# The second product of a token MLP: order of the wide, low and narrow matmuls within a step

## Chip, cores and metric

The kernel runs on one core of a Trainium2 chip. The metric is the device time of one execution in microseconds; the median of three runs stands for a kernel.

## What is computed

The block is a pre-norm layer: linear attention with a learned feature map, then an MLP across the tokens. With x of 2048 tokens by 512 channels:

```python
h = x + A(layernorm(x))            # attention, 32 heads of 16
n = layernorm(layernorm(h))        # one norm of the block, one of the MLP
u = gelu(n.T @ w1 + b1)            # (512, 1792): w1 is (2048, 1792)
y = u @ w2 + b2                    # (512, 2048): w2 is (1792, 2048)
out = h + y.T
```

The change lies in `u @ w2`, the last stage.

## The kernel before, in words

The work comes in three stretches: attention with its projections, the first product of the MLP (it starts while attention still runs), and the second product from about 379 us on.

The second product is written as Winograd's form of Strassen's method: a block of two by two becomes seven products of sums and differences instead of eight. The blocks on the one side are halves of a 256-row piece of w2 by two token tiles; on the other side they are halves of the matching piece of u by two halves of 256 channels. `STEPS` (line 767) runs over 8 token pairs `sp` and, in each, 7 pieces `p` of the hidden dimension. So a token pair has seven steps, and a step has seven products, listed in `PROD` (line 817) as (slice of the weights, slice of u, bank, half). For the last token pair `LAST` (line 819) is used.

Every operand is split in two parts, a high one, rounded to the type `float32r` that the matmuls take, and a low one with what is missing. A product needs high by high, high by low and low by high. The tile of u holds high and low beside each other, 256 columns each. So where `half` is None, one matmul of 512 columns does high weights by both parts (line 823, here called wide), and one of 256 columns adds low weights by the high part (line 824, here called low). Where `half` is 0 or 1 the two results of a wide matmul shall be added to one half of a bank at once, and three matmuls of 256 columns are used (line 827, here called narrow). In `PROD` five products are of the first kind and two, both in the third bank, are narrow: sixteen matmuls a step. In `LAST` all seven are narrow, 21 a step.

`products` (line 830) takes a list of steps: for each product it goes through the steps. The first five steps of a token pair are issued one by one; the sixth and seventh (the last three in the last pair) are issued together, product by product, so that the banks are finished one after the other (line 861). Behind them ACT and DVE add the banks up and GpSimd's queue adds the result to the output in memory.

The weights arrive by a DMA on the SP queue two steps at a time (`load_w2`, line 775). DVE makes the sums (lines 785 to 787), ACT the high part of all seven slices in one instruction (line 796, three buffers `whi`), DVE the low part (line 805, two buffers `wlo`). These are issued at the head of each group of two steps, for groups further ahead. The parts of u lie in `un` for the first two pieces and in `uf` for the others. The order of TensorE, DVE and ACT is the order of the code (line 839); each engine waits only where its operands or buffers make it wait. There are eight banks, and a token pair takes six in turn.

Of the kernel before, what the change touches and what calls it, by code (L numbers as in the profile page):

```python
# [22 lines left out]
NP = NF // 2  # L23
# [13 lines left out]
def block_kernel(ctx: ExitStack, tc: tile.TileContext, x, xT, wT, phic, wo, w1, b1, w2, b2,  # L37
                 kvmask, ident_in, out):
    nc = tc.nc
# [685 lines left out]
    U, UB, far = {}, {}, {}  # L725
# [43 lines left out]
    RAW, WH, AW = {}, {}, {}  # L769
# [7 lines left out]
    def sums_w2():  # L777

        g = done["sums"]
        if g == NGR:  # L780
            return
        done["sums"] += 1
        load_w2(g)
        raw = RAW[g]
        nc.vector.tensor_add(raw[:, 0:2], raw[:, 1].unsqueeze(1).to_broadcast([P, 2, GRP * P]), raw[:, 2:4])
        nc.vector.tensor_add(raw[:, 5], raw[:, 1], raw[:, 2])
        nc.vector.tensor_add(raw[:, 6], raw[:, 4], raw[:, 5])

    def hi_w2():

        g = done["hi"]
        if g == NGR:
            return
        done["hi"] += 1
        WH[g] = ws.tile([P, 7, GRP * P], F32R, name="whi", bufs=3)
        nc.scalar.activation(WH[g], RAW[g], AF.Copy)  # L796

    def lo_w2():

        g = done["lo"]  # L800
        if g == NGR:
            return
        done["lo"] += 1
        wl_ = ws.tile([P, 7, GRP * P], F32R, name="wlo", bufs=2)
        nc.vector.tensor_sub(wl_, RAW[g], WH[g])  # L805
        for i, step in enumerate(STEPS[g * GRP:(g + 1) * GRP]):
            AW[step] = WH[g][:, :, i * P:(i + 1) * P], wl_[:, :, i * P:(i + 1) * P]
# [10 lines left out]
            (4, 3, 5, None))  # L818
    LAST = ((2, 1, 0, 0), (5, 5, 0, 1), (0, 0, 1, 0), (1, 4, 1, 1), (3, 6, 2, 0), (6, 2, 2, 1), (4, 3, 3, 0))

    def product(o, half, a, b, first, start, stop):
        if half is None:
            nc.tensor.matmul(o, a[0], b, start=start, stop=stop, skip_group_check=True)  # L823
            nc.tensor.matmul(o[:, 0], a[1], b[:, 0], start=False, stop=stop, skip_group_check=True)  # L824
            return
        for i, (x, y) in enumerate(((0, 0), (0, 1), (1, 0))):
            nc.tensor.matmul(o[:, half], a[x], b[:, y], start=start and first and i == 0, stop=stop and i == 2,  # L827
                             skip_group_check=True)

    def products(sp, ps, order):  # L830
        for a, b, bk, half in order:
            for p in ps:
                wh_, wl_ = AW[sp, p]
                product(bank[bk], half, (wh_[:, a], wl_[:, a]), UB[p, b], half != 1, p == 0, p == NP - 1)

    def flat(a):
        return a.rearrange("p k d -> p (k d)")
# [3 lines left out]
    for n, (sp, p) in enumerate(STEPS):  # L841
        t = 2 * sp
        last = t + 2 == NT
        if n % GRP == 0 and p < NP - 1:
            lo_w2()
            hi_w2()
            sums_w2()
        if p == 0:
            bank = []
            for _ in range(6):  # L850
                pool = (ps_f, ps_q, ps_b, ps_b)[n_bank % 8 // 2]
                bank.append(pool.tile([P, 2, HD], F32, name="py", tag="pu"))
                n_bank += 1
        order = LAST if last else PROD
        run_on = 3 if last else 2
        if p < NP - run_on:
            products(sp, [p], order)
            continue
        if p < NP - 1:
            continue  # L860
        products(sp, range(NP - run_on, NP), order)
        e = uo.tile([P, 2, HD], F32, name="e")
        u2 = uo.tile([P, HD], F32, name="u2", bufs=1)
        u3 = uo.tile([P, HD], F32, name="u3")
        if not last:
            ot = uo.tile([P, 2, 2, HD], F32, name="ot", bufs=1)
            low = uo.tile([P, 3, HD], F32, name="low", bufs=1)
            nc.scalar.activation(e[:, 1], bank[0][:, 0], AF.Copy)
            for i in range(3):
                nc.scalar.activation(low[:, i], bank[3 + i][:, 1], AF.Copy)  # L870
            nc.vector.tensor_add(e[:, 1], bank[0][:, 1], e[:, 1])
            nc.vector.tensor_sub(u2, bank[1][:, 0], e[:, 1])
            nc.vector.tensor_add(u2, bank[1][:, 1], u2)
            nc.vector.tensor_sub(u3, u2, bank[2][:, 0])
            nc.vector.scalar_tensor_tensor(e[:, 0], bank[2][:, 1], -1.0, u2, op0=ALU.mult, op1=ALU.subtract)

            def out_block(i, h, o, add):
                nc.vector.scalar_tensor_tensor(ot[:, i, h], o, b2s[:, t + i:t + i + 1], add, op0=ALU.add, op1=ALU.add)  # L878

            out_block(0, 0, bank[2][:, 1], u3)  # L880
            out_block(0, 1, bank[3][:, 0], u3)
            nc.gpsimd.dma_start(out[t * P:(t + 1) * P, :], flat(ot[:, 0]), accum_op=ALU.add)  # L882
            if n % GRP == 0:
                lo_w2()
                hi_w2()
            out_block(1, 0, bank[4][:, 0], e[:, 0])
            out_block(1, 1, bank[5][:, 0], e[:, 1])
            nc.gpsimd.dma_start(out[(t + 1) * P:(t + 2) * P, :], flat(ot[:, 1]), accum_op=ALU.add)
            nc.gpsimd.dma_start(out[t * P:(t + 1) * P, HD:D], low[:, 0], accum_op=ALU.add)
            nc.gpsimd.dma_start(out[(t + 1) * P:(t + 2) * P, :], flat(low[:, 1:3]), accum_op=ALU.add)  # L890
            if n % GRP == 0:
                sums_w2()
            continue

        hb = [hp.tile([P, 2, HD], F32, name=f"hb{i}") for i in range(2)]
        for i in range(2):
            nc.sync.dma_start(flat(hb[i]), out[(t + i) * P:(t + i + 1) * P, :])
            nc.vector.tensor_scalar(hb[i], hb[i], b2s[:, t + i:t + i + 1], None, op0=ALU.add)
        nc.scalar.activation(e[:, 1], bank[0][:, 0], AF.Copy)
        nc.vector.tensor_add(hb[1][:, 1], bank[0][:, 0], hb[1][:, 1])  # L900
        nc.vector.tensor_sub(u2, bank[0][:, 1], e[:, 1])
        nc.vector.tensor_sub(hb[1][:, 0], hb[1][:, 0], u2)
        nc.vector.tensor_sub(u3, u2, bank[1][:, 0])
        nc.vector.tensor_add(hb[0], hb[0], u3.unsqueeze(1).to_broadcast([P, 2, HD]))
        nc.vector.tensor_add(hb[0][:, 0], bank[1][:, 1], hb[0][:, 0])
        nc.vector.tensor_sub(hb[1][:, 0], hb[1][:, 0], bank[1][:, 1])
        nc.vector.tensor_add(hb[0][:, 1], bank[2][:, 0], hb[0][:, 1])
        nc.sync.dma_start(out[t * P:(t + 1) * P, :], flat(hb[0]))
        for k, o, q in ((0, bank[2][:, 1], nc.scalar), (1, bank[3][:, 0], nc.sync)):
            nc.vector.tensor_add(hb[1][:, k], o, hb[1][:, k])  # L910
            q.dma_start(out[(t + 1) * P:NT * P, k * HD:(k + 1) * HD], hb[1][:, k])
# [49 lines left out]
```

## Time and profile before

| | |
|---|---|
| median of three runs | 523.97 us (523.72 to 524.6) |
| the profiled execution | 524.12 us |
| its span, first to last instruction | 522.3 us |
| mean granted clock of TensorE | 0.999 |
| TensorE matmuls | 516.6 us busy, 3379 instructions |
| weight loads | 436.5 us, 3379 |
| DVE, ACT, GpSimd | 386.5, 282.3 and 239.8 us |

Times in the rows are in microseconds from the start of the span unless marked ns. PE is TensorE's matmuls, PEld its weight loads, which run beside them. The duration of a matmul includes its way through the array, in which the next has begun already, so the rate of matmuls is read from the distance of their starts or ends and not from their durations. The names around `<-` are the tiles written and read.

### The profile page before, as it was taken

How to read it: one execution, taken by the hardware profiler on the slowest of the kernel's cores; microseconds unless marked ns; L12 is line 12 of the kernel's file. 1: busy time of each engine (PE TensorE's matmuls, PEld its weight loads, DVE VectorE, ACT ScalarE, POOL GpSimd, SP SyncE). 2: the span in 40 equal slices, each digit the busy share in tenths (PEclk: the TensorE clock that was granted, in tenths of full speed). 3: DMA queues.
4: the chain of work that ended last, by engine and by line, in shares of the span. 5: the costliest groups of instructions: out<-in, count | busy, mean ns of one | idle time of the engine just before them, and what ended most of it. 6: DMA issues, size and time to landing. Idle time of an engine off the chain costs nothing.

```text
span 522.3 us, 8917 instructions
## 1 busy us (share of the span) xinstructions
PE 516.6 (99%) x3379; PEld 436.5 (84%) x3379; DVE 386.5 (74%) x681; ACT 282.3 (54%) x496; POOL 239.8 (46%) x188
## 2 busy tenths in 40 slices
PE   9999999999999999999999999999999999999997
PEld 8788888887877767888788888888899999999997
DVE  6893999986899998863227424725779888988985
ACT  6999853424246876666956423625453434434430
POOL 2579799985999999874424000000002112212220
PEclk9999999999999999999999999999999999999999
DMA  8544210020131324343333354532215687678734
GB/s 317 198 122 122 80 43 22 1 80 24 30 113 60 102 86 136 105 130 130 102 100 102 102 179 143 176 92 77 76 45 115 158 191 161 120 164 186 163 43 82
DMA packets 36298, 58.52 MB, mean 112 GB/s; under 512 B 3744, under 2 KB 19360, under 8 KB 36256
## 3 DMA queue, kind: packets, MB, share of 16 engines
q1 hardware_dynamic: 31936, 51.37, 31.2%
q0 software_dynamic: 4032, 6.42, 9.1%
q8 instruction: 26, 0.43, 0.3%
q10 hardware_dynamic: 288, 0.17, 0.1%
q14 instruction: 16, 0.13, 0.1%
HBM read 46.81 MB, written 11.14 MB: 111 GB/s over the span
## 4 chain that ended last, share of the span: by engine, by line
PE 90%; POOL 7%; DVE 2%; issue 1%; ACT 0%; POOLq 0%
PE pu L65 12%; PE pu L66 12%; PE pu L67 11%; PE py L823 11%; PE py L827 10%; PE py L824 6%; PE pv L66 3%; PE pv L67 3%; PE pv L65 3%; PE pk_ps L65 2%; PE pk_ps L67 2%; PE pk_ps L66 2%; POOL ez L447 2%; POOL eq L465 2%; PE po L67 2%; PE po L65 2%
## 5 line engine op out<-in xcount | busy, mean ns | idle before, releaser
L66 PE MATMUL pu<-hs,whi 128*128 128x512 f32 x224 | 87.6, 391 | 1.2 <-POOL hs L61 1.2
L65 PE MATMUL pu<-hs,whi 128*128 128x512 f32 x224 | 87.4, 395 | 0.0
L67 PE MATMUL pu<-hs,wlo 128*128 128x512 f32 x224 | 87.0, 389 | 0.0
L606 DVE TENSOR_TENSOR wlo<-wraw,whi 128x512 fp32r<-128x512 f32 x56 | 43.8, 784 | 53.2 <-ACT whi L614 53.0
L882 POOL DMA_DIRECT2D out<-ot x7 | 6.2, 887 | 153.9 <-DVE ot L878 153.9
L796 ACT ACTIVATE whi<-wraw 128x1792 fp32r<-128x1792 f32 x28 | 47.4, 1701 | 46.7 <-PE py L823 20.6
L805 DVE TENSOR_TENSOR wlo<-wraw,whi 128x1792 fp32r<-128x1792 f32 x28 | 56.5, 2022 | 12.1 <-PE py L824 8.9
L823 PE MATMUL py<-uf,whi 128*128 128x512 f32 x175 | 63.4, 399 | 0.0
L614 ACT ACTIVATE whi<-wraw 128x512 fp32r<-128x512 f32 x56 | 34.9, 627 | 49.6 <-PE pu L66 45.3
L65 PEld LDWEIGHTS pu<-hs,whi 128*128 128x128 f32 x224 | 42.1, 188 | 10.9 <-issue 2.5
L66 PEld LDWEIGHTS pu<-hs,whi 128*128 128x128 f32 x224 | 42.1, 188 | 10.4 <-POOL hs L61 2.1
L67 PEld LDWEIGHTS pu<-hs,wlo 128*128 128x128 f32 x224 | 42.1, 188 | 8.6
L824 PE MATMUL py<-uf,wlo 128*128 128x256 f32 x175 | 49.2, 281 | 0.0
L447 POOL TENSOR_TENSOR ez<-eq,zB 128x1024 f32<-128x1024 f32 x16 | 38.4, 2400 | 4.4 <-ACT zB L494 4.4
L827 PE MATMUL py<-uf,whi 128*128 128x256 f32 x210 | 39.0, 283 | 0.0
L823 PEld LDWEIGHTS py<-uf,whi 128*128 128x128 f32 x175 | 33.0, 188 | 6.8
L200 POOL TENSOR_TENSOR pk<-pk,sk 128x1024 f32<-128x1024 f32 x16 | 31.0, 1940 | 7.6 <-DVE sk L199 5.0
L534 ACT ACTIVATE pht<-tn 128x512 f32<-128x512 f32 x32 | 17.4, 596 | 30.2 <-PE tn L532 30.2
L827 PEld LDWEIGHTS py<-uf,whi 128*128 128x128 f32 x210 | 32.4, 189 | 1.4
L824 PEld LDWEIGHTS py<-uf,wlo 128*128 128x128 f32 x175 | 33.1, 189 | 0.0
L465 POOL TENSOR_TENSOR eq<-eq,w 128x1024 f32<-128x1024 f32 x16 | 32.3, 2017 | 1.3 <-DVE w L462 1.2
L61 POOL TENSOR_TENSOR hs<-hn,hs 128x512 fp32r<-128x512 f32 x16 | 21.6, 1350 | 23.7 <-ACT hs L60 23.7
(179 smaller groups left out, 1344.2 us busy)
## 6 DMA issues: line engine op xcount, KB each, us to landing
wraw<-in_w SPq DMA_DIRECT2D x56, 256.0 KB, 2.8
wraw<-in_w SPq DMA_DIRECT2D x28, 512.0 KB, 4.1
xraw<-in_xT SPq DMA_DIRECT2D x16, 256.0 KB, 2.8
xh<-in_x SPq DMA_DIRECT2D x16, 256.0 KB, 2.6
h<-in_x SPq DMA_DIRECT2D x16, 256.0 KB, 2.7
out<-h SPq DMA_DIRECT2D x16, 256.0 KB, 2.4
out<-ot POOLq DMA_DIRECT2D x14, 256.0 KB, 4.8
wraw<-in_wT SPq DMA_DIRECT2D x12, 256.0 KB, 4.4
```

Source lines behind the costliest of these rows:

```text
L65: nc.tensor.matmul(o, ah, bh, start=first, stop=False)
L66: nc.tensor.matmul(o, ah, bl, start=False, stop=False)
L67: nc.tensor.matmul(o, al, bh, start=False, stop=last)
L447: nc.gpsimd.tensor_mul(EZ[t], EQ[t], zB)
L465: nc.gpsimd.tensor_mul(heads(EQ[t]), heads(EQ[t]), W[t].rearrange("p g c h -> p (g c h)").unsqueeze(2).to_broadcast([P, 2 * H, DH]))
L606: LO.append(nc.vector.tensor_sub(wl_, raw, wh_).ins)
L614: nc.scalar.activation(wh_, raw, AF.Copy)
L796: nc.scalar.activation(WH[g], RAW[g], AF.Copy)
L805: nc.vector.tensor_sub(wl_, RAW[g], WH[g])
L823: nc.tensor.matmul(o, a[0], b, start=start, stop=stop, skip_group_check=True)
L824: nc.tensor.matmul(o[:, 0], a[1], b[:, 0], start=False, stop=stop, skip_group_check=True)
L827: nc.tensor.matmul(o[:, half], a[x], b[:, y], start=start and first and i == 0, stop=stop and i == 2, skip_group_check=True)
```

## The change

In steps two to five of a token pair, the five wide matmuls of a step are issued in a row, then its five low ones, then the six narrow ones. The first step stays as it was. The helper that walks the sixth and seventh step together changes too: for each product it now issues the wide matmuls of both steps and then the low ones of both. Every matmul keeps its operands and its bank. The code, cut to its core:

```diff
-    def product(o, half, a, b, first, start, stop):
-        if half is None:
-            nc.tensor.matmul(o, a[0], b, start=start, stop=stop, skip_group_check=True)
-            nc.tensor.matmul(o[:, 0], a[1], b[:, 0], start=False, stop=stop, skip_group_check=True)
-            return
...
     def products(sp, ps, order):
         for a, b, bk, half in order:
-            for p in ps:
-                wh_, wl_ = AW[sp, p]
-                product(bank[bk], half, (wh_[:, a], wl_[:, a]), UB[p, b], half != 1, p == 0, p == NP - 1)
+            if half is None:
+                for low in range(2):
+                    for p in ps:
+                        wide(sp, p, a, b, bk, low)
+            else:
+                for p in ps:
+                    narrow(sp, p, a, b, bk, half)
+
+    def wide(sp, p, a, b, bk, low):
+        w, u = AW[sp, p][low][:, a], UB[p, b]
+        o, u = (bank[bk][:, 0], u[:, 0]) if low else (bank[bk], u)
+        nc.tensor.matmul(o, w, u, start=p == 0 and not low, stop=p == NP - 1, skip_group_check=True)
...
+    def step(sp, p, order):
+        for low in range(2):
+            for a, b, bk, half in order:
+                if half is None:
+                    wide(sp, p, a, b, bk, low)
+        for a, b, bk, half in order:
+            if half is not None:
+                narrow(sp, p, a, b, bk, half)
...
         run_on = 3 if last else 2
+        if p == 0:
+            products(sp, [p], order)
+            continue
         if p < NP - run_on:
-            products(sp, [p], order)
+            step(sp, p, order)
             continue
```

On TensorE, the second step of the first token pair began like this (`py` are the banks, `un1` is the second piece of u, `whi` and `wlo` the parts of the weights):

```order
L823 MATMUL py_4137<-un1_3199,whi_4110 128x512
L824 MATMUL py_4137<-un1_3199,wlo_4112 128x256
L823 MATMUL py_4138<-un1_3199,whi_4110 128x512
L824 MATMUL py_4138<-un1_3199,wlo_4112 128x256
L827 MATMUL py_4139<-un1_3199,whi_4110 128x256 x2
L827 MATMUL py_4139<-un1_3199,wlo_4112 128x256
L827 MATMUL py_4139<-un1_3199,whi_4110 128x256 x2
L827 MATMUL py_4139<-un1_3199,wlo_4112 128x256
L823 MATMUL py_4140<-un1_3199,whi_4110 128x512
L824 MATMUL py_4140<-un1_3199,wlo_4112 128x256
```

Two more pairs of wide and low follow, for the banks 4141 and 4142. The same step now, with the lines of the changed file:

```order
L834 MATMUL py_4137<-un1_3199,whi_4110 128x512
L834 MATMUL py_4138<-un1_3199,whi_4110 128x512
L834 MATMUL py_4140<-un1_3199,whi_4110 128x512
L834 MATMUL py_4141<-un1_3199,whi_4110 128x512
L834 MATMUL py_4142<-un1_3199,whi_4110 128x512
L834 MATMUL py_4137<-un1_3199,wlo_4112 128x256
L834 MATMUL py_4138<-un1_3199,wlo_4112 128x256
L834 MATMUL py_4140<-un1_3199,wlo_4112 128x256
L834 MATMUL py_4141<-un1_3199,wlo_4112 128x256
L834 MATMUL py_4142<-un1_3199,wlo_4112 128x256
L838 MATMUL py_4139<-un1_3199,whi_4110 128x256 x2
L838 MATMUL py_4139<-un1_3199,wlo_4112 128x256
```

The second narrow product ends the step. All five wide matmuls moved to its front, and the narrow ones from its middle to its end.

The second place is the joint run of steps six and seven in the same pair, here two of its six banks, before (`whi_4130` and `wlo_4175` are step six's weights, `whi_4177` and `wlo_4216` step seven's):

```order
L823 MATMUL py_4140<-uf_4073,whi_4130 128x512
L824 MATMUL py_4140<-uf_4073,wlo_4175 128x256
L823 MATMUL py_4140<-uf_4098,whi_4177 128x512
L824 MATMUL py_4140<-uf_4098,wlo_4216 128x256
L823 MATMUL py_4141<-uf_4063,whi_4130 128x512
L824 MATMUL py_4141<-uf_4063,wlo_4175 128x256
L823 MATMUL py_4141<-uf_4088,whi_4177 128x512
L824 MATMUL py_4141<-uf_4088,wlo_4216 128x256
```

And now:

```order
L834 MATMUL py_4140<-uf_4073,whi_4130 128x512
L834 MATMUL py_4140<-uf_4098,whi_4177 128x512
L834 MATMUL py_4140<-uf_4073,wlo_4175 128x256
L834 MATMUL py_4140<-uf_4098,wlo_4216 128x256
L834 MATMUL py_4141<-uf_4063,whi_4130 128x512
L834 MATMUL py_4141<-uf_4088,whi_4177 128x512
L834 MATMUL py_4141<-uf_4063,wlo_4175 128x256
L834 MATMUL py_4141<-uf_4088,wlo_4216 128x256
```

Step seven's wide matmul changed places with step six's low one. DVE, ACT, GpSimd and SP have the rows that they had, in the same order.

More of the change, by code (lines that the diff above doesn't have):

```diff
@@ L819, in block_kernel, with narrow @@
     LAST = ((2, 1, 0, 0), (5, 5, 0, 1), (0, 0, 1, 0), (1, 4, 1, 1), (3, 6, 2, 0), (6, 2, 2, 1), (4, 3, 3, 0))
-    def product(o, half, a, b, first, start, stop):
-        if half is None:
-            nc.tensor.matmul(o, a[0], b, start=start, stop=stop, skip_group_check=True)
-            nc.tensor.matmul(o[:, 0], a[1], b[:, 0], start=False, stop=stop, skip_group_check=True)
-            return
-        for i, (x, y) in enumerate(((0, 0), (0, 1), (1, 0))):
-            nc.tensor.matmul(o[:, half], a[x], b[:, y], start=start and first and i == 0, stop=stop and i == 2,
-                             skip_group_check=True)
     def products(sp, ps, order):
         for a, b, bk, half in order:
-            for p in ps:
-                wh_, wl_ = AW[sp, p]
-                product(bank[bk], half, (wh_[:, a], wl_[:, a]), UB[p, b], half != 1, p == 0, p == NP - 1)
+            if half is None:
[9 more added lines that the diff above has]
+        nc.tensor.matmul(o, w, u, start=p == 0 and not low, stop=p == NP - 1, skip_group_check=True)
+    def narrow(sp, p, a, b, bk, half):
+        for i, (x, y) in enumerate(((0, 0), (0, 1), (1, 0))):
+            nc.tensor.matmul(bank[bk][:, half], AW[sp, p][x][:, a], UB[p, b][:, y], start=p == 0 and half == 0 and i == 0,
+                             stop=p == NP - 1 and i == 2, skip_group_check=True)
+    def step(sp, p, order):
[6 more added lines that the diff above has]
+                narrow(sp, p, a, b, bk, half)
     def flat(a):
```

## Prediction

> **What bounds the kernel now.** I read the busy shares first, then the chain of work that ended last. The first row gives each engine's busy time and its share of the span, the second the clock that TensorE was granted in 40 slices, the third the shares of the chain.
>
> ```profile
> PE 516.6 (99%) x3379; PEld 436.5 (84%) x3379; DVE 386.5 (74%) x681; ACT 282.3 (54%) x496; POOL 239.8 (46%) x188
> PEclk9999999999999999999999999999999999999999
> PE 90%; POOL 7%; DVE 2%; issue 1%; ACT 0%; POOLq 0%
> ```
>
> TensorE is busy 99% of 522.3 us and carries 90% of the chain, at full clock throughout. So only the pace of its matmuls can move the end, unless the change makes it wait. The changed code runs from 379.5 us to about 501 us, so I look at the pace there, and at what two plain rows of matmuls cost elsewhere.
>
> The chain in order of time, in the third token pair (start, length, line; L823 is a wide matmul of 512 columns, L824 the 256 columns with the low weights behind it, L827 the narrow ones of 256 columns; a piece runs from the end of the matmul ahead to its own end):
>
> ```profile
> 410.87 1.44 PE py L827 x12
> ...
> 417.63 0.71 PE py L827 x6
> 418.35 0.23 PE py L823
> 418.58 0.12 PE py L824
> 418.70 0.24 PE py L823
> 418.94 0.12 PE py L824
> 419.06 0.23 PE py L823
> 419.29 0.12 PE py L824
> 419.41 0.23 PE py L823
> 419.64 0.12 PE py L824
> 419.76 0.24 PE py L823
> 420.00 0.12 PE py L824
> 420.12 0.71 PE py L827 x6
> ...
> 425.09 0.71 PE py L827 x6
> ...
> 428.28 1.44 PE py L827 x12
> ```
>
> From the six narrow ones at 417.63 to those at 425.09 are three steps: 7.46 / 3 = 2.487 us each. The six take 0.71 to 0.72 (417.63 to 418.35), so five pairs of wide and low take 2.487 - 0.715 = 1.772, or **354 ns a pair**. There is no gap in the chain: this is all pace.
>
> Now the same two kinds apart. In the first product, 512 columns follow 512 columns (timeline of TensorE: start, length of one, line):
>
> ```profile
> 340.04 0.39 PE L65 MATMUL pu<-hs,whi 128*128 128x512 f32 x1
> 340.27 0.39 PE L66 MATMUL pu<-hs,whi 128*128 128x512 f32 x1
> 340.50 0.39 PE L67 MATMUL pu<-hs,wlo 128*128 128x512 f32 x1
> 340.72 0.39 PE L65 MATMUL pu<-hs,whi 128*128 128x512 f32 x1
> ...
> 349.56 0.39 PE L65 MATMUL pu<-hs,whi 128*128 128x512 f32 x1
> ```
>
> The length of one overlaps its successor; the distance of starts is the pace. Between 340.04 and 349.56 lie 42 matmuls: 9.52 / 42 = **226.7 ns** each. The last pair is narrow throughout, and the chain there is one piece:
>
> ```profile
> 501.46 17.66 PE py L827 x147
> ```
>
> 17.66 / 147 = **120.1 ns** for 256 columns. A wide and a narrow one, each among its own kind, come to 226.7 + 120.1 = 346.8 ns. The pair in alternation costs 354: **7.4 ns too many**, for going from wide to narrow and back once. That excess is what the reader is to see; nothing else in the stage is idle time that could be won.
>
> The excess is not even. The first pair behind the narrow ones takes 0.35 (418.35 to 418.70), the second 0.36 (to 419.06). So one excursion from a narrow row to a wide one and back, standing alone, seems to cost 3 or 4 ns (350 less 346.8), and those that follow closely cost more.
>
> **The change, part by part.** The count of matmuls, their shapes, weights and weight loads stays. DVE, ACT, GpSimd and the DMA queues issue the same instructions in the same order. Only TensorE's order changes, in two places; the last pair has no wide product, so there both orders are one.
>
> Steps two to five. Before, a step has five excursions (two ahead of the narrow ones, three behind). After, it has one: five wide, then five low and six narrow, eleven of 256 columns in a row. Taking each removed excursion at the mean 7.4 ns: 4 x 7.4 = 30 ns. Taking the whole step as five times the mean less one lone excursion: 5 x 7.4 - 3.5 = 33.5 ns. There are 28 such steps (four in each of seven pairs): 0.83 to 0.94 us.
>
> Steps six and seven run together, and there wide, low, wide, low becomes wide, wide, low, low in five places: five excursions fewer in each pair, 5 x 7.4 = 37 ns, over seven pairs 0.26 us. Lone or not, these five remaining ones might be cheaper too, which would make it 10 x 7.4 - 5 x 3.5 = 57 ns and 0.40 us. The words of the change do not name this part, but it is about a quarter of the sum.
>
> Together **1.09 to 1.34 us**; I take 1.25, nearer the upper, because the chain shows the first excursion of a step at 0.35 in every step. If the excursions that remain were free, it would be 28 x 37 + 7 x 74 = 1.55 us.
>
> The edits that I cost at nothing. The low weights have two buffers, and DVE refills one while TensorE reads the other. The tightest place that I find is in the timeline (the bracket tells how long DVE waited, and for whom):
>
> ```profile
> 424.49 2.03 DVE L805 TENSOR_TENSOR wlo<-wraw,whi 128x1792 fp32r<-128x1792 f32 x1 [0.71 <-PE py L824]
> ```
>
> ```profile
> 426.70 0.40 PE L823 MATMUL py<-uf,whi 128*128 128x512 f32 x1
> 426.71 0.19 PEld L824 LDWEIGHTS py<-uf,wlo 128*128 128x128 f32 x1
> ...
> 427.05 0.40 PE L823 MATMUL py<-uf,whi 128*128 128x512 f32 x1
> 427.06 0.19 PEld L824 LDWEIGHTS py<-uf,wlo 128*128 128x128 f32 x1
> ```
>
> The new low weights are there at 424.49 + 2.03 = 426.52. Step six starts at 426.70, and step seven's first low load at 427.06: a margin of 0.54 us. What releases the buffer stays the last matmul of a step (a low one before, a narrow one with low weights after), so DVE starts as before; the step in between gets 0.03 shorter, and the first load of the new low weights moves one place back, behind the second wide one. The margin becomes about 0.6. In steps two to five the low weights are wanted later than now, behind five wide ones (5 x 0.227 = 1.1 us instead of 0.23), so that margin grows. The high weights are released by the last but one matmul in both orders. If a margin did go, TensorE would wait and every matmul behind it, once for each lack.
>
> What no row shows is ten matmuls in a row that each write another bank; the first product changes its bank at every third one, where 0.22 to 0.23 is seen on either side (340.50 to 340.72, 340.27 to 340.50). By the resolution of those rows a change of bank costs between -4 and +4 ns. A step has eleven such changes where it had six (the joint steps have as many as before): at most 5 x 4 ns x 28 = 0.56 us either way, and since the rows agree I take zero.
>
> [...]
>
> **The rivals.**
>
> No change. The excess may belong to the stage and not to the alternation: more traffic on the memory that feeds the array. The windows (length, busy time of PE, PEld, DVE, ACT, POOL, then clock, DMA share and GB/s) show the stage to be denser:
>
> ```profile
> 335.00:360.00 25.00, 25.00 (x112) 20.68 (x112) 8.13 (x14) 8.72 (x15) 0.00 (x0) 1.00 0.44 127
> 397.74:499.35 101.61, 101.61 (x657) 92.18 (x657) 91.12 (x134) 42.57 (x42) 20.20 (x24) 1.00 0.73 158
> ```
>
> DVE is busy 8.13 of 25 us in the first and 91.12 of 101.61 in the second, and the DMA share goes from 0.44 to 0.73. If that slows wide matmuls by 7 ns wherever they stand, nothing is won: 523.97 us. Against it: the narrow ones of the same stage take 0.715 / 6 = 119 ns, no more than the last pair's, and the pairs differ by place within a step, the same in each.
>
> More than counted. If a wide one in a row also sheds what the changes of bank cost now, the 0.56 us come on top of 1.55: 2.1 us, 521.9 us. For it speaks only that no row forbids it.
>
> Slower. The loads of weights become the bound in the long row of narrow matmuls. Each load lasts 0.19 us in the rows above, 0.07 longer than a narrow matmul's 0.12 slot. In alternation every other slot is a wide one, long enough to hide it; five lows in a row with five different slices have none. Were the load's whole length exclusive, each of the five would cost 0.07 more: 28 x 0.35 = 9.8 us, with the 35 places of the joint steps 35 x 0.07 = 2.4, less the gain: about 535 us. It decides as soon as a load cannot overlap the one ahead of it. Against it stands the row of 147 narrow ones at 120.1 ns, in which two loads of three bring another slice; loads of 0.19 at a distance of 0.12 overlap there already. [...]
>
> **How the numbers follow.** The profiled execution took 524.12 us, 0.15 above the median 523.97. 524.12 - 1.25 = 522.87 for such an execution; the median to expect is 523.97 - 1.25 = **522.7**. Chances: the forecast, a gain of 0.8 to 1.6 us, 0.64; no change (within 0.3 us) 0.18; more than 1.6 us 0.10; slower 0.08. The range takes in the bounds of the forecast, the larger gain and the unchanged time with the spread of the runs: 521.6 to 524.1. What it leaves out is the slower rival and little else. Faster by over 0.2% means over 1.05 us, about what a measurement of this kernel can tell from no change. The forecast's centre lies just beyond it; I give three quarters of it, 0.48, to that side: faster 0.48 + 0.10 = 0.58, within 0.16 + 0.18 = 0.34, slower 0.08.
>
> **What would show it.** In the changed kernel's chain a step should last 2.455 us instead of 2.487; wide matmuls should start 227 ns apart within a row of five, the eleven behind them 119 to 120 apart, and a whole pair should take about 17.23 us where it takes 17.41 (from the twelve at 410.87 to those at 428.28). If a step stays at 2.487 and the wide ones stand 234 apart, the stage's traffic is the cause. If lows stand more than 125 apart, the loads are. A new wait of TensorE for DVE's L805 (by its new number) would make the margins wrong. I would also be wrong if the joint steps showed no gain while the others did, since both rest on the same excess.

## The result, and the profile after

The changed kernel takes 523.28 us (median of 22 runs, 522.68 to 523.65) against 523.99 (22 runs of the kernel before beside it): 0.71 us less. The ratio is 0.9984, with a 95% interval of 0.9978 to 0.9990. The forecast was 522.7, a gain of 1.25.

The busy shares and the chain of the changed kernel's page, its span being 521.8 us:

```profile
PE 515.2 (99%) x3379; PEld 435.8 (84%) x3379; DVE 386.0 (74%) x681; ACT 282.0 (54%) x496; POOL 239.6 (46%) x188
PEclk9999999999999999999999999999999999999999
PE 89%; POOL 7%; DVE 2%; DMA 1%; issue 1%; SPq 0%; ACT 0%; POOLq 0%
```

The same counts, and TensorE busy 1.4 us less. Nothing else took its place in the chain of the second product. That chain, again in the third token pair (L834 is now every wide and low matmul, L838 every narrow one):

```profile
411.06 1.44 PE py L838 x12
...
416.00 2.81 PE py L834 x16
418.81 0.72 PE py L838 x6
419.53 1.75 PE py L834 x10
421.29 0.72 PE py L838 x6
422.00 1.75 PE py L834 x10
423.76 0.72 PE py L838 x6
424.48 1.75 PE py L834 x10
426.23 0.72 PE py L838 x6
426.95 1.39 PE py L834 x8
428.35 1.44 PE py L838 x12
...
497.47 1.44 PE py L838 x12
```

Three steps lie between the sixes at 418.81 and 426.23: 7.42 / 3 = 2.473 us, where 2.487 stood before and 2.455 was forecast. The five wide and five low take 1.75, not 1.77. The twelves are the joint run of steps six and seven, one in each token pair, so their distance is the time of a pair: (497.47 - 411.06) / 5 = 17.28 us. Before, the last of them stood here:

```profile
497.90 1.44 PE py L827 x12
```

(497.90 - 410.87) / 5 = 17.41. A pair is won 0.126 us, and seven of them 0.88. That is within the interval of the timed runs (0.0010 to 0.0022 of 524 us is 0.5 to 1.15 us), and it is the sharper number: it repeats from pair to pair, while what lies ahead of the stage differs from one execution to the next. The first twelve began at 393.79 in this profile, and in those of the experiments below anywhere from 392.84 to 394.13.

How the five wide ones stand within a row is seen in the timeline of TensorE (start, length of the row, its count at the end):

```profile
416.90 1.32 PE L834 MATMUL py<-un,whi 128*128 128x512 f32 x5
418.06 0.76 PE L834 MATMUL py<-un,wlo 128*128 128x256 f32 x5
418.65 0.40 PE L838 MATMUL py<-un,whi 128*128 128x256 f32 x2
```

From the first wide to the first low one are 1.16 us, 232 ns for each of the five and not 226.7. The five lows take 0.59, 118 each.

TensorE has no row among the waits of this stage. DVE waits for its buffers as before, 10.8 us in all where it was 10.6 (total, times, longest). In the kernel before and in the changed one:

```profile
DVE wlo L805 <- PE py L824: 8.9, 9, 1.5
DVE wlo L805 <- PE py L827: 1.7, 1, 1.7
```

```profile
DVE wlo L805 <- PE py L838: 9.4, 9, 1.5
DVE wlo L805 <- PE py L834: 1.4, 4, 0.4
```

### The profile page after: what moved, and what is told of

It is laid out like the page before. It is cut to its first block, busy times and chain, and to the rows that moved or that the text cites. A ratio compares the mean times of both kernels' runs of the same rounds, so it can differ in the third digit from the quotient of the medians.

```text
span 521.8 us, 8917 instructions
## 1 busy us (share of the span) xinstructions
PE 515.2 (99%) x3379; PEld 435.8 (84%) x3379; DVE 386.0 (74%) x681; ACT 282.0 (54%) x496; POOL 239.6 (46%) x188
## 4 chain that ended last, share of the span: by engine, by line
PE 89%; POOL 7%; DVE 2%; DMA 1%; issue 1%; SPq 0%; ACT 0%; POOLq 0%
PE py L834 16%; PE pu L65 12%; PE pu L66 12%; PE pu L67 11%; PE py L838 10%; PE pv L66 3%; PE pv L67 3%; PE pv L65 3%; PE pk_ps L65 2%; PE pk_ps L67 2%; PE pk_ps L66 2%; POOL ez L447 2%; POOL eq L465 2%; PE po L66 2%; PE po L65 2%; PE po L67 2%
## 5 line engine op out<-in xcount | busy, mean ns | idle before, releaser
L834 PE MATMUL py<-uf,whi 128*128 128x512 f32 x175 | 49.8, 395 | 0.0
L838 PE MATMUL py<-uf,whi 128*128 128x256 f32 x210 | 39.1, 283 | 0.0
L838 PEld LDWEIGHTS py<-uf,whi 128*128 128x128 f32 x210 | 32.8, 192 | 0.0
L834 PEld LDWEIGHTS py<-uf,wlo 128*128 128x128 f32 x175 | 28.5, 189 | 5.0
L204 POOL TENSOR_TENSOR zacc<-zacc,pk 128x1024 f32<-128x1024 f32 x13 | 31.3, 2405 | 0.6
L834 PEld LDWEIGHTS py<-uf,whi 128*128 128x128 f32 x175 | 29.1, 190 | 2.7
```

What stands on the lines that cost most here:

```text
L204: nc.gpsimd.tensor_add(zacc, zacc, PK[t])
L834: nc.tensor.matmul(o, w, u, start=p == 0 and not low, stop=p == NP - 1, skip_group_check=True)
L838: nc.tensor.matmul(bank[bk][:, half], AW[sp, p][x][:, a], UB[p, b][:, y], start=p == 0 and half == 0 and i == 0, stop=p == NP - 1 and i == ...
```

## The experiments

Two questions were open: which part won what, and why a step won 14 ns instead of 33. The theory that I formed from the trace is a **run-in**: behind narrow matmuls the first wide ones of a row are slow, and only later ones reach 226.7 ns. The rivals are the prediction's: traffic of the stage, and changes of bank.

**The steps alone.** The joint run gets its old order back:

```diff
-                for low in range(2):
-                    for p in ps:
+                for p in ps:
+                    for low in range(2):
                         wide(sp, p, a, b, bk, low)
```

> Steps two to five in the new order, the joint steps in the old one. By the trace of after a new step takes 2.473 us against 2.487, so 28 x 14 ns = 0.39 us are to be won here and the rest of the 0.86 us that the traces show belongs to the joint steps: the token pair should take 17.407 - 4 x 0.014 = 17.35 us, about 523.6 us in all. By the prediction's own sizes (33 ns a step) the pair would take 17.27.

523.55 us, ratio 0.9994 (0.9985 to 1.0002). Its chain:

```profile
392.94 1.44 PE py L838 x12
...
497.06 1.44 PE py L838 x12
```

(497.06 - 392.94) / 6 = 17.353 us a pair: 0.053 won, as the trace of the changed kernel had said and not as the prediction had. The timed runs of this kernel and of the next one cannot be told from no change, since both intervals include 1; what they won is read from the traces.

**The joint run alone.** Steps two to five get their old order back:

```diff
         if p < NP - run_on:
-            step(sp, p, order)
+            products(sp, [p], order)
             continue
```

> Only the joint steps six and seven in the new order (wide, wide, low, low), steps two to five as before. If the gain of the parts adds up, the pair takes 17.407 - 0.046 (joint) - 0.026 (first step, which begins behind two low ones instead of one) = 17.335 us, about 523.5 us in all: more from the part that the words of the change do not name than from the four steps that they do. By the prediction's sizes this part wins 0.037 to 0.057 a pair, 17.35 to 17.37.

523.60 us, ratio 0.9993 (0.9984 to 1.0002). Its chain:

```profile
394.13 1.44 PE py L838 x12
...
412.90 2.78 PE py L834 x16
415.69 0.71 PE py L838 x6
...
498.13 1.44 PE py L838 x12
```

(498.13 - 394.13) / 6 = 17.333: 0.073 won. The parts add up, 0.053 + 0.073 = 0.126. Most of what the joint run wins lies behind the twelve, from its end to the next six. That stretch holds the last three banks of the joint run and the first two pairs of the next step; it takes 2.78 here and 2.83 in the first experiment:

```profile
429.09 2.83 PE py L834 x16
```

So the order in the joint run, which the change's name does not mention, gave more than half of the gain, and part of it falls in step one, whose own code stayed the same.

**Rows of two.** Steps two to five in another order:

```diff
     def step(sp, p, order):
-        for low in range(2):
-            for a, b, bk, half in order:
-                if half is None:
+        wides = [o for o in order if o[3] is None]
+        for i in range(0, len(wides), 2):
+            for low in range(2):
+                for a, b, bk, half in wides[i:i + 2]:
                     wide(sp, p, a, b, bk, low)
```

> The changed kernel with the wide ones of steps two to five in rows of two (wide, wide, low, low, twice, then wide, low, then the six narrow ones). Theory of the run-in: the first five wide matmuls behind narrow ones stand 233, 236, 228, 233, 231 apart and only later ones 226.7, and two low ones behind two wide ones win 12 ns back (116 + 112 in the joint steps of after); so two by two costs 697 for four where the row of five costs 350.6 a pair: a step takes about 2.46 us, 10 ns less than a row of five, and the pair 17.24. Rival, the prediction's count of excursions at 7.4 ns each: three instead of one, a step 15 ns longer than after, the pair 17.34.

523.19 us, ratio 0.9987 (0.9978 to 0.9996).

```profile
393.07 1.44 PE py L838 x12
...
496.75 1.44 PE py L838 x12
```

(496.75 - 393.07) / 6 = 17.280, the pair of the changed kernel to the nanosecond. Neither side was right. Three excursions to wide matmuls cost no more over the pair than one, so the prediction's price of 7.4 ns for each is wrong. But the saving that I had worked out from the joint run's rows of two did not come either.

**Rows of ten.** Two steps that share a group of weights are taken together (steps two and three, and four and five, in every other token pair; three and four in the others):

```diff
-    def step(sp, p, order):
+    def step(sp, ps, order):
         for low in range(2):
-            for a, b, bk, half in order:
-                if half is None:
-                    wide(sp, p, a, b, bk, low)
+            for p in ps:
+                for a, b, bk, half in order:
+                    if half is None:
+                        wide(sp, p, a, b, bk, low)
...
-            step(sp, p, order)
+            if last or sp % 2 == 0 and p in (1, 4):
+                step(sp, [p], order)
+            elif n % GRP == 1:
+                step(sp, [p - 1, p], order)
             continue
```

> The changed kernel with rows of ten: where two of steps two to five share a group of weights, the ten wide ones of both stand in a row, then ten low ones, then twelve narrow ones. Run-in: the sixth to the tenth wide one stand 226.7 apart, so two steps take about 4.946 - 5 x 5.6 = 4.918 us and one excursion less saves another 7 to 10 ns. Rival, traffic on the memory or changes of bank slow every wide one of this stage to 232.6: the sixth to tenth stay at 232 to 233, and two steps take 4.94 us.

A single run took 522.9 us. The kernel was then timed:

> The kernel with rows of ten again, timed. Its trace had token pairs of 17.24 and 17.26 us against 17.28 of the changed kernel and 17.41 of the kernel before, so over seven pairs 1.06 us less than before and 0.20 less than the changed kernel: about 522.9 us, ratio 0.998, if nothing ahead of the stage differs.

522.63 us (7 runs, 522.45 to 523.4), ratio 0.9975 (0.9964 to 0.9987). The timeline of TensorE in the timed kernel's profile, in the second token pair:

```profile
403.60 2.46 PE L834 MATMUL py<-uf,whi 128*128 128x512 f32 x10
405.89 1.35 PE L834 MATMUL py<-uf,wlo 128*128 128x256 f32 x10
407.08 0.40 PE L838 MATMUL py<-uf,whi 128*128 128x256 f32 x2
```

Ten wide ones take 405.89 - 403.60 = 2.29 us. By their starts in this trace the first five stand 233, 236, 228, 233 and 230 ns apart, as in the changed kernel, and the other five 227, 227, 226, 227 and 227. That is the pace of the first product, in the middle of this stage's traffic and with another bank at every matmul. So the wide ones did as the run-in says and not as the rival does. The two steps together were a miss for both: 4.926 us, where the run-in with one excursion less had 4.91 and the rival 4.94. They win 20 ns on the changed kernel's 4.946, about what one row loses, and nothing beside it for the excursion. The kernel's pairs, from the twelves of the joint run:

```profile
392.84 1.44 PE py L838 x12
...
496.34 1.44 PE py L838 x12
```

(496.34 - 392.84) / 6 = 17.25 us: 0.03 a pair less than the changed kernel, 0.2 us in all (20 ns in a pair with one row of ten, 40 in a pair with two). Against the kernel before it is clearly faster, 0.25%. Against the changed kernel the timed intervals overlap (0.9964 to 0.9987 and 0.9978 to 0.9990), so the claim that it beats this one as well rests on the traces.

**No refills.** The functions that load and split the weights stop after the first groups, and later groups use the first two again. This leaves out the loads of weights from there on and most of the stage's DVE and ACT work, and computes the output from wrong weights:

```diff
-        if g == NGR:
+        if g >= 3:
             return
         done["sums"] += 1
...
+        if g >= 2:
+            for i, step in enumerate(STEPS[g * GRP:(g + 1) * GRP]):
+                AW[step] = AW[STEPS[g % 2 * GRP + i]]
+            return
```

> The changed kernel without the refills of the weights: after the third group no weights are loaded and summed, and after the second no high and low parts are made; the later groups use the first two again, so the result of the block is left wrong. TensorE's instructions stay. Traffic theory (the prediction's first rival): with DVE, ACT and the DMA queue nearly quiet in this stage, the wide ones go at 226.7 from the first of a row on, a step takes 2.453 us. Run-in: nothing changes, 2.473 us a step and 17.28 us a pair.

A single run took 523.53 us. First the window over six pairs (columns as in the prediction), of the changed kernel and of this one, then the chain, where L842 is the narrow matmuls' line:

```profile
397.74:499.35 101.61, 101.61 (x662) 92.63 (x661) 91.71 (x136) 42.61 (x42) 20.47 (x24) 1.00 0.73 158
397.74:499.35 101.61, 101.61 (x662) 92.61 (x662) 21.41 (x51) 8.07 (x21) 20.18 (x24) 1.00 0.42 55
```

```profile
393.62 1.44 PE py L842 x12
...
497.30 1.44 PE py L842 x12
```

DVE falls from 91.71 to 21.41 us, ACT from 42.61 to 8.07, the DMA share from 0.73 to 0.42, and the pair stays at (497.30 - 393.62) / 6 = 17.280. GpSimd's work and a DMA share of 0.42 are left; but apart from GpSimd's 20 us the stage is now no denser than the first product (DMA share 0.44, DVE 8.13 of 25 us), where wide matmuls stood 226.7 ns apart. The prediction's traffic rival is out.

**Other orders.** Two kernels with a different order in each of steps two to five, to see whether any beats a long row:

> The changed kernel with another order in each of steps two to five (W wide, L low, n one narrow matmul): WWLLWWLLWLnnnnnn, WWLLnnnWWLLnnnWL, WWWLLLWWLLnnnnnn, WLnWLnWLnWLnWLnn. If what costs is only the run-in behind narrow ones, the longest rows are best and all four take 2.473 us or more, the last, with five lone wide ones each behind two narrow ones, the longest, 2.49 to 2.5. If a few 256-column matmuls between wide ones cost nothing and only a settled row of them does, the second and third are down at 2.46.

> As the kernel with orders a, with WWLLWWLLWnnnnnnL, WWLnWWLnWLLnnnnL, WWWLLnWWLLnnnnnL and WWWWLLLLWLnnnnnn. The same theories: run-in alone gives 2.473 us or more for all of them; the first differs from orders a's first only by one low matmul that stands behind the narrow ones, and should take the same time.

A single run of each took 523.69 and 522.74 us. The chains, orders a first:

```profile
393.86 1.44 PE py L838 x12
...
497.54 1.44 PE py L838 x12
```

```profile
393.03 1.44 PE py L838 x12
...
496.59 1.44 PE py L838 x12
```

17.280 and 17.260 us a pair. By the starts of the steps in the traces, steps two to five take 2.464, 2.469, 2.466 and 2.481 us in the one and 2.464, 2.473, 2.475 and 2.463 in the other, and the joint run 4.937 and 4.922 where the changed kernel has 4.924. So the run-in as I had it, which allowed none below 2.473 and gave five lone wide ones 2.49 to 2.5, is not the whole rule. One order of a step does not even have one price: the plain rows of two took 2.464 us as step two and 2.473 as steps three to five of the same pair. What one step wins can be given back in a later one: there the joint run took 4.933, which are the 9 ns of step two again. The pairs of these two kernels differ by 20 ns, and what carries such differences from step to step stays open.

## Why the prediction was right or wrong

**The bound** was right. TensorE's pace sets this stage, it waits for nothing there, and the margins of the weights' buffers held.

**The term of steps two to five was mis-sized**: 30 to 33.5 ns a step, 0.83 to 0.94 us, against 14 ns and 28 x 0.014 = 0.39 us. The step that failed is the price of a wide matmul "among its own kind". I took 226.7 ns from the middle of a row hundreds long and gave it to a row of five. The trace of before shows what the beginning of a row costs. This is a row of twelve of 512 columns in the attention's projections, behind matmuls of 256 columns (timeline of TensorE; four rows of one matmul each are left out at each mark):

```profile
11.68 1.11 PE L129 MATMUL pk_ps<-wkl,xs 128*128 128x256 f32 x8
12.62 0.40 PE L65 MATMUL pk_ps<-wkh,xs 128*128 128x512 f32 x1
...
13.79 0.39 PE L67 MATMUL pk_ps<-wkh,xs 128*128 128x512 f32 x1
...
14.92 0.39 PE L66 MATMUL pk_ps<-wkl,xs 128*128 128x512 f32 x1
```

From 12.62 to 13.79 are five distances, by their starts 233, 236, 228, 233 and 231 ns; from 13.79 to 14.92 the next five, 226 to 227. In the changed kernel's trace the five distances of a row are the same 233, 236, 228, 233 and 231 ns, give or take 1, and the lows behind them 113, 119 and then 120. That is 27 ns over five settled wide ones, of which the first two lows give 8 back. By the time of a step, 2.473 - 2.455, a row of five loses 18 ns, and the pair of steps with a row of ten loses no more. A row of five never gets out of its run-in. Before, a step lost 2.487 - 2.455 = 32 ns, and 32 less 18 is the 14 that were won.

The price of a lone excursion, 3.5 ns, was a reading of one pair. By their starts the five pairs of a step before take 350, 361, 350, 361 and 349 ns, so the cost does not grow with each further turn; and the one excursion that is left, a row of five, costs 18.

**The joint run** was priced at 37 to 57 ns a pair and is worth 73 with what it does to step one (second experiment). By the starts of the steps the joint run itself goes from 4.970 to 4.924 us, 46 ns, which is inside the forecast. Step one goes from 2.490 to 2.463; for those 26 ns the prediction has no term. I had noticed that the change does more than its name says, but had not asked what the next step finds in front of it.

**The sum** came out at 0.88 us by the traces and 0.71 by the medians, against 1.09 to 1.34. By the medians the gain lies between the prediction's "no change" (within 0.3) and its forecast (0.8 to 1.6), where it had given no chance, and a gain of over 0.2%, to which it gave 0.58, did not come (0.16%). The sign was right, and so was that the excess lies in the order of TensorE's matmuls and not in the stage around them. That each turn between wide and narrow has its price was not. One term was twice too large and another about a third too small, so that part of the error cancelled; that is luck.

**The rivals.** Traffic is refuted by the kernel without refills. Changes of bank cost nothing visible: the settled wide ones in a row of ten change theirs every time. The loads do not bound the row of lows, which stand 113 to 120 apart. My sign for the traffic, wide ones 234 apart, was badly chosen: the run-in gives nearly the same distance, and only a longer row or a quieter stage tells the two apart. The Trainium skill, page "TensorE: Matmul & The Clock Gate", section "Back-to-back issue gap", has a formula from the columns alone, columns / 2.4 + 2.5 ns; it calls this the isolated gap of a single matmul and says that in a stream of loads and matmuls both set the spacing. An estimate by that formula is 215.8 ns for 512 columns, below the 226 to 227 of the settled rows here. It has no term for the order, with which the same matmuls take 17.41, 17.35, 17.33, 17.28 and 17.25 us a pair.

## What to carry to other kernels

A pace read in the middle of a long row is the price of a long row. Before giving it to a short one, look in the same trace at the first few instructions behind a change of kind. And where a change is worth a tenth of a per cent, take it from the period of its own stage in the trace, which repeated to about 0.01 us here, rather than from whole times, which scatter by 1 us here, much of it ahead of the stage.

## What the hardware showed that I had not expected

A row of matmuls of 512 columns behind a settled row of 256-column ones needs five to reach its pace (233, 236, 228, 233, 231, then 226 to 227 ns), in the attention's projections as in the second product, and there with the refills of the weights and without them. Other neighbours give other beginnings: in the trace of before the first product's long row starts at 250.15 us with 336, 236, 228, 233, 231 and then 226, behind the matmuls of L551, and a row behind the 128-column ones of L532 at 204.48 us with 314, 233, 231 and then 226. The cost is not a sum of prices per turn. One row of five and one row of ten lose about 18 ns against settled rows, and so do rows of two, two and one in three of their four steps, while five single turns lose 32. Why the first five are slow was not found.
